# Batch 0's second feed-forward product as seven products, row-block pair by row-block pair

## The chip, the cores and the metric

The kernel runs on one core of a Trainium2 chip. The metric is the device time of one execution in microseconds. Before the change it is 704.37 us, the median of 3 runs (704.09 to 704.53). The profiled execution took 704.29 us; its span in the trace is 702.5 us, with TensorE's clock granted at 0.998 throughout.

## What is computed

```python
# x: (8, 8, 512, 64), state: (8, 8, 32, 64), float32
scores  = scale * x @ state^T          # per batch and head: 512 x 32
a       = softmax(scores)
xread   = a @ state                    # 512 x 64
scores2 = scale * state @ x^T          # 32 x 512
sread   = softmax(scores2) @ x         # 32 x 64
t = concat([xread, sread], axis=2)     # (8, 8, 544, 64)
t = t.transpose(0, 2, 1, 3).reshape(8 * 544, 512)
h = t @ w_in                           # w_in: (512, 2048)
g = h / (1 + exp(-1.702 h))
out = g @ w_out                        # w_out: (2048, 512)
```

The weights arrive as 64-bit floats and are rounded to 32 bits in the kernel. Everything else is 32-bit.

## The kernel before the change, in words

**Engines.** Each engine takes its instructions strictly in the order in which the code emits them. There is no scheduler: the order was written out by hand. TensorE does the products, VectorE (DVE in the profile) most of the element-wise work, ScalarE (ACT) the activations and most copies out of PSUM, and SyncE (SP) issues all transfers.

**Weights.** `PIECES` lists 32 pieces, 16 of w_in and then the 16 row blocks of w_out (128 rows by 512 columns, loaded as pairs of words). Piece *i* is loaded by `load_weight`. The row blocks of w_out use the four rooms of `later` in turn, so block piece *i*+4 can only be loaded when piece *i* has been rounded. Rounding builds the 32-bit number from the two words. Its VectorE steps are `mask` (L214: the exponent bits), a clamp and shift of these (L222 and L223, for w_out), `fraction` (L232), and in `round_b` the sign (L243), the low word (L246) and the final product (L250). For w_in the clamp is two ScalarE activations instead (L225 and L226), up to `AHEAD` = 3 pieces ahead. For w_out no step is taken ahead of its piece.

**Batches 0 and 1** are interleaved, since the weights are still arriving. For a quarter *c* of the 2048 columns, `att_M` multiplies w_in with the state (L327), and `up_x` multiplies the result with the normalized scores (L539) and applies the activation on ScalarE (L542), one block *f* of 128 columns at a time: blocks 0 to 15 of both batches.

**Batch 0's second product** is the loop over *f* at L1302. Each turn rounds row block *f* of w_out and then runs `down` for the four row groups: four products of 128 x 128 with 128 x 512 (L557), added up in four PSUM banks over the 16 turns. Between turns stand the state reads (`att_eT`, `att_sread`, `att_srT`), two `att_M`, and the last eight `up_x` of batch 1. Each row group is then copied out by ScalarE (L564) and stored.

**Batches 1 to 7** take their second product in seven half-size products in place of eight (Winograd's form of Strassen's scheme). With the left matrix in quarters a11 to a22 and w_out in quarters B11 to B22, the sums are T1 = B12 - B11, T2 = B22 - T1, T3 = B22 - B12, T4 = B21 - T2 on the right (`T_of`, L1285), and S1 = a21 + a22, S2 = S1 - a11, S3 = a11 - a21, S4 = a12 - S2 on the left (`s12`, L580 and L581; `s3`, L586). `strassen_two` splits most of the seven once more (`strassen_low`, L703), with sums of quarters of quarters: `low_made` and `low_away` make those of the right side, the latter in a room that is then stored to DRAM (L663), and `low_third` (L1285 too) makes the third in place. For batch 1 the first two products, P1 and P2, are taken whole (L752), and the following P5 in parts. Into P1 and P2 of batch 1 the attention of batch 2 is hooked: its scores (L327 into the banks o_2 and o_3), their transposes (`att_blocks`, L358), maxima (`att_s_max`, L365 and L366) and exponentials (`att_s_exp`, L384, ScalarE).

So on VectorE the order after the last row block is: T1, the sums of quarters, S1, S2, T2, S3, T3, more sums of quarters, the transposes of batch 2's x (`turn_x`, L163), T4 and its sums, the sums of S1 and S2 (first seven of L759), the transposes and maxima of batch 2, and then the sum of P2 and P1 (next L759, `osb`), which frees the PSUM bank o_1 that the second part of P5 writes.

Of the kernel before, what the change touches and what calls it, by code (L numbers as in the profile page):

```python
# [10 lines left out]
FP32 = mybir.dt.float32  # L11
# [3 lines left out]
ALU = mybir.AluOpType  # L15
# [5 lines left out]
def kernel(  # L21
# [71 lines left out]
    def att_ps(shape, name):  # L93
        return psA.tile(shape, FP32, tag="att", name=name)
# [7 lines left out]
    free = [gpool.tile([P, 2, S], FP32, name=f"g_{i}") for i in range(HF)]  # L102

    sums = konst.tile([P, 3, HF * HN], FP32, name="sums")
    T1, T2, T4 = (sums[:, i].rearrange("p (f n) -> p f n", f=HF) for i in range(3))
    free += [
        sums[:, 1 + i // 2, 2 * S * (i % 2) : 2 * S * (i % 2 + 1)].rearrange("p (k t) -> p k t", k=2) for i in range(4)
    ]
    later = konst.tile([P, 8, S], FP32, name="later")

# [59 lines left out]
    w_out = konst.tile([P, NF, DM], FP32, name="w_out")  # L170
    w_in_words, w_out_words = moe_w_in.bitcast(I32), moe_w_out.bitcast(I32)

    PIECES = [("i", c, k) for c in range(NFC) for k in range(NPR)] + [("o", f) for f in range(NF)]
    raw, power, begun = {}, {}, {}
    AHEAD = 3

# [39 lines left out]
    def round_a(i):  # L216

        if i not in power:
            mask(i)
        sc = power[i]  # L220
        if PIECES[i][0] == "o":
            nc.vector.tensor_scalar(sc, sc, most, least, ALU.min, ALU.max)  # L222
            nc.vector.tensor_scalar(sc, sc, -least, 8.0, ALU.add, ALU.mult)  # L223
            return
        nc.scalar.activation(out=sc.bitcast(FP32), in_=sc, func=AF.Relu, bias=edge[0], scale=-8.0)  # L225
        nc.scalar.activation(out=sc, in_=sc.bitcast(FP32), func=AF.Relu, bias=edge[1], scale=-1.0)  # L226
# [8 lines left out]
    def round_b(i, ahead, follows):  # L235


        if i not in begun:
            fraction(i)
        dst = begun.pop(i)  # L240
        lo, hi = words(i)
        sc = power.pop(i)
        nc.vector.scalar_tensor_tensor(sc, hi, -0x80000000, sc, ALU.bitwise_and, ALU.bitwise_or)  # L243
        powers_to(ahead)

        nc.vector.scalar_tensor_tensor(dst, lo, 2.0**-32, dst.bitcast(I32), ALU.mult, ALU.add)  # L246
        del raw[i]
        if follows and i + 1 in raw:
            fraction(i + 1)
        nc.vector.scalar_tensor_tensor(dst, dst, 2.0**-20, sc.bitcast(FP32), ALU.mult, ALU.mult)  # L250
# [19 lines left out]
    def round_to(n, ahead=AHEAD):  # L270

        nin = NFC * NPR
        while done["b"] < min(n, len(PIECES)):
            i = done["b"]
            powers_to(i + 1)
            round_b(i, min(i + 1 + ahead, max(nin, i + 1)), i + 1 < nin and (i + 1 < n or i >= NPR))
            done["b"] += 1
            while done["b"] > NPR and done["load"] < len(PIECES) and before(done["load"]) < done["b"]:
                load_weights(done["load"] + 1)
# [80 lines left out]
    def att_s_max(b):  # L360
        a = A[b]
        a["mx2"] = []
        for g in range(NG):
            mx = apool.tile([P, 1], FP32, tag="mx2", name=f"mx2_{b}_{g}", bufs=4)
            nc.vector.tensor_reduce(out=mx, in_=a["s"][g], axis=AX.X, op=ALU.max, negate=True)  # L365
            nc.vector.tensor_scalar(mx, mx, scale, None, ALU.mult)  # L366
            a["mx2"].append(mx)
# [164 lines left out]

    G = {}

    def up(key, f, ntok, lhs, rhs, spare=False):
        hps = att_ps([P, ntok], f"h_{key}_{f}") if spare else psH.tile([P, ntok], FP32, tag="h", name=f"h_{key}_{f}")
        n = len(lhs)
        for i in range(n):
            nc.tensor.matmul(hps, lhs[i], rhs[i], start=(i == 0), stop=(i == n - 1))  # L539
        if f % 2 == 0:  # L540
            G[key, f // 2] = free.pop(0)
        nc.scalar.activation(out=G[key, f // 2][:, f % 2, :ntok], in_=hps, func=AF.Gelu_apprx_sigmoid)  # L542

    def up_x(b, f, spare=False):
        c, o = divmod(P * f, FC)
        m = A[b]["M", c]
        up(b, f, S, [m[:, g, o : o + P] for g in range(NG)], [A[b]["aT"][:, g] for g in range(NG)], spare)

    O = {}

    def down(key, r, fs, dst, last):

        if fs[0] == 0:
            O[key, r] = bank_o[r]
        ops = O[key, r]
        for f in fs:
            nc.tensor.matmul(  # L557
                ops, G[key, f // 2][:, f % 2, P * r : P * (r + 1)], w_out[:, f], start=(f == 0), stop=(f == NF - 1)
            )
            if last and f < HF and f % 2:  # L560
                free.append(G.pop((key, f // 2)))
        if fs[-1] == NF - 1:
            osb = opool.tile([P, DM], FP32, tag="osb", name=f"osb_{key}_{r}")
            nc.scalar.copy(osb, ops)  # L564
            nc.sync.dma_start(dst, osb)


    S1, S2 = (later[:, 4 * i : 4 * i + 4].rearrange("p f n -> p (f n)").rearrange("p (f t) -> p f t", f=HF) for i in range(2))

# [632 lines left out]
    def rounds(n):  # L1202
        round_to(done["b"] + n)
# [47 lines left out]
    def turn(b, c, then, n=()):  # L1251

        for i in range(nper):
            if i == nper - 1 and then:
                att_M(*then)
            up_x(b, nper * c + i)
            if i < len(n):
                rounds(n[i])
# [4 lines left out]
    round_to(3 * NPR)  # L1263
    turn(1, 1, (0, 2), [1, 1])
    round_to(4 * NPR)
    att_s_max(0)
    att_s_max(1)
    turn(0, 2, (0, 3))
    room = apool.tile([P, NPR, S], FP32, tag="xT", name="e2_01")
    att_s_exp(0, room[:, :NG])  # L1270
    att_s_exp(1, room[:, NG:])
    rounds(1)
    att_s_norm(0)
    att_s_norm(1)
    up_x(0, 3 * nper)
    up_x(0, 3 * nper + 1)
    up_x(0, 3 * nper + 2, True)
    up_x(0, 3 * nper + 3, True)
    rounds(1)


    B11, B12, B21, B22 = (w_out[:, HF * i : HF * (i + 1), HN * k : HN * (k + 1)] for i in range(2) for k in range(2))
# [15 lines left out]
        low_keep(k, room)  # L1298


    rest = list(range(2 * nper, NF))
    for f in range(NF):  # L1302
        rounds(1)
        round_to(NFC * NPR + f + 1)
        if f == NF - 1:

            up_x(1, rest.pop(0))
        for r in range(SCH):
            down(0, r, [f], out_x[0, r], r == SCH - 1)
        if f == 0:  # L1310
            for b in range(2):
                for g in range(NG):
                    att_eT(b, g)
        if f == 1:

            att_sread(0)
            att_sread(1)
            att_M(1, 2, True)
            att_M(1, 3)
        if f == 2:  # L1320
            att_srT(0)
            att_srT(1)
        if f == 2 or f % 2 == 1 and 1 < f < NF - 1:
            up_x(1, rest.pop(0))
        if f == HF:
            load_state(2)
            load_x_squares(2)
        if f == NF - 2:
            T_of(T1, B12, B11)
            low_away(6, B22)  # L1330
            low_made(5, T1, 1)
            for u in range(NU - 1):
                s12(1, u, S)
            T_of(T2, B22, T1)
            low_third(T1)
            for u in range(NU - 1):
                s3(1, u, S)
            T_of(B12, B22, B12)
            low_away(3, T3)
            low_third(T3)  # L1340
        if f == NF - 1:
            turn_x(2)
            low_made(2, T2, 0)
    s12(1, NU - 1, S)
    s3(1, NU - 1, S)

    def out_of(b):
        return lambda r, n: out_x[b, r, :, n].rearrange("r q n -> q r n")

    for b in range(1, B):  # L1350
        if b > 1:
            ahead = {"P1.1": [(up_strassen(b, S, *parts_x(b), A[b]["sums"]), ())]}
            if b == 2:
                ahead["P1.5"] = [low_sums(B21, low_a)[2], (low_keep, (1, turn_rooms[0]))]
                ahead["P1.6"] = [(low_third, (B21,))]
        else:
            ahead = {
                "P1a": [(low_third, (B22,)), (T_of, (T4, B21, T2)), (low_third, (T2,)), (low_away, (4, T4)), (low_third, (T4,))]
            }
        if b + 1 < B:  # L1360
            hooks = hooks_next(b + 1)
        else:

            steps, left, right = sr_sums()
            order = (
                ("P5.6", 2), ("P6.1", 3), ("P6.3", 6), ("P6.4", 7), ("P7.5", 8), ("P7.6", 9), ("P4.1", 16, 17), ("P4.5", 18, 19),
            )
            hooks = {name: [steps[i] for i in n] for name, *n in order}
            hooks["P3.7"] = [(low_third, (T1,))]
            beside = steps[10:16] + [(low_third, (t,)) for t in (B11, B21, T2, T3, T4, B22)]  # L1370
            ahead["P2.1"] = [steps[i] for i in (0, 1)]
            ahead["P2.3"] = [steps[i] for i in (4, 5)]
        for name, first in ahead.items():
            hooks[name] = first + hooks.get(name, [])
        a4 = {}

        at = hooks.setdefault("run", [])
        k = 3 if b + 1 < B else 0
        at[k:k] = [(low4_load, (a4,))]
        strassen_two(b, out_of(b), hooks, a4)  # L1380
        if b + 2 < B:
            load_state(b + 2)
            load_x_squares(b + 2)
# [35 lines left out]
```

## Time and profile before

| what | busy or time |
|---|---|
| span | 702.5 us |
| TensorE matmul | 689.3 us, 98% |
| VectorE | 569.4 us, 81% |
| ScalarE | 301.9 us, 43% |
| rounding of w_out on VectorE | 66.6 to 130.1 us of the span |
| batch 0's second product on TensorE | 78.2 to 153.3 us of the span |
| first part of P5 of batch 1 on TensorE | 170.05 us of the span |

The busy share of TensorE is an average over stages: an engine that is busy 98% of the whole span is not by that the only one that limits each stage, so the stage that changes has to be read by itself. Times below are counted from the start of the span. A 32-bit matmul is two records in the trace, so a turn of the loop at L1302 (4 matmuls) shows as 8 records.

### The profile page before, as it was taken

What the parts mean: (1) busy time and instruction counts of PE and PEld (TensorE: products, weight loads), DVE (VectorE), ACT (ScalarE), POOL (GpSimd) and SP (SyncE); (2) the same over time, 40 slices, a digit from 0 to 9 for tenths busy, and PEclk for the clock granted to TensorE, in tenths of its full rate; (3) what the DMA queues carried; (4) which work ended last, traced back from release to release, by engine and by line L of the source; (5) the groups of instructions that cost most, each with busy time, mean ns of one, the idle gap of its engine ahead of it and who ended that gap; (6) DMA issues with size and microseconds to landing.
All of it is one profiled execution on the core that took longest, in us unless ns stands there. A gap on an engine that the chain in (4) does not pass through costs nothing.

```text
span 702.5 us, 13525 instructions
## 1 busy us (share of the span) xinstructions
PE 689.3 (98%) x5263; PEld 560.1 (80%) x5263; DVE 569.4 (81%) x1187; ACT 301.9 (43%) x677; POOL 0.8 (0%) x8
## 2 busy tenths in 40 slices
PE   8989999999999999999999999999999999999996
PEld 3433444457998799889989899889988998999995
DVE  6999799998879989697969886988878795887540
ACT  5686520014336533654355533753375236422420
POOL 0000000000000000000000000000000000000000
PEclk9999999999999999999999999999999999999999
DMA  8921246326524484427451664157433840251001
GB/s 220 383 67 56 91 151 151 123 80 200 172 75 94 140 239 141 88 66 235 146 115 31 174 218 116 24 134 231 142 55 106 235 142 16 71 148 53 16 0 31
DMA packets 105807, 87.39 MB, mean 124 GB/s; under 512 B 64784, under 2 KB 84752, under 8 KB 105744
## 3 DMA queue, kind: packets, MB, share of 16 engines
q1 hardware_dynamic: 105744, 86.53, 42.0%
q8 instruction: 42, 0.69, 0.4%
q14 instruction: 21, 0.17, 0.1%
HBM read 68.94 MB, written 17.56 MB: 123 GB/s over the span
## 4 chain that ended last, share of the span: by engine, by line
PE 89%; DVE 6%; DMA 2%; SPq 1%; ACT 1%; issue 0%; DVEq 0%; ACTq 0%
PE low L703 28%; PE o L703 15%; PE o L1123 13%; PE o L557 8%; PE h L539 7%; PE upx L1123 5%; PE M L327 4%; PE o L600 2%; PE o L752 2%; PE upw L1123 2%; PE sr L515 1%; PE upx_sr L1123 1%; DMA w_out<-in_moe_w_in_dram 1%; DMA out_dram<-osb_sr 1%; PE o L327 1%; SPq L148 1%
## 5 line engine op out<-in xcount | busy, mean ns | idle before, releaser
L703 PE MATMUL low<-w_out,g 128*128 128x128 f32 x416 | 54.3, 276 | 0.0
L703 PEld LDWEIGHTS low<-w_out,g 128*128 128x128 f32 x416 | 50.5, 192 | 4.5 <-issue 3.4
L1123 PE MATMUL o<-ta,M 128*128 128x256 f32 x192 | 49.9, 382 | 0.0
L1123 PE MATMUL upx<-aT,M 128*128 128x256 f32 x192 | 49.3, 379 | 0.0
L703 PE MATMUL low<-low,g 128*128 128x128 f32 x336 | 43.3, 275 | 0.4 <-ACT o L712 0.4
L703 PEld LDWEIGHTS low<-low,g 128*128 128x128 f32 x336 | 40.3, 192 | 0.5 <-ACT o L712 0.5
L1123 PEld LDWEIGHTS o<-ta,M 128*128 128x128 f32 x192 | 35.5, 190 | 6.0 <-ACT g L1169 1.6
L1123 PEld LDWEIGHTS upx<-aT,M 128*128 128x128 f32 x192 | 36.0, 190 | 4.7
L542 ACT ACTIVATE g<-h 128x512 f32<-128x512 f32 x24 | 14.0, 591 | 54.5 <-PE h L539 54.5
L474 ACT COPY M<-M 128x512 f32<-128x512 f32 x59 | 30.7, 596 | 14.8 <-PE M L327 14.7
L703 PE MATMUL low<-sums,later 128*128 128x128 f32 x280 | 35.8, 275 | 0.0
L1129 ACT ACTIVATE g<-o 128x512 f32<-128x512 f32 (+1 forms) x56 | 31.3, 559 | 10.2 <-PE o L1123 10.2
L703 PEld LDWEIGHTS low<-sums,later 128*128 128x128 f32 x280 | 33.6, 192 | 0.1
L327 PE MATMUL M<-w_in,stT 64*32 64x512 f32 x472 | 32.0, 594 | 0.0
L539 PE MATMUL h<-low,M 128*128 128x512 f32 x64 | 29.5, 597 | 1.7 <-DVE low L420 1.7
L1123 PE MATMUL o<-ta,ms 128*128 128x256 f32 x120 | 30.8, 379 | 0.0
L539 PE MATMUL h<-aT,M 128*128 128x512 f32 x64 | 28.7, 599 | 1.4 <-ACT M L474 1.4
L557 PE MATMUL o<-w_out,g 128*128 128x512 f32 x64 | 28.5, 594 | 0.0
L557 PE MATMUL o<-w_out,sums 128*128 128x512 f32 x64 | 28.3, 592 | 0.0
L1129 ACT ACTIVATE g<-g 128x512 f32<-128x512 f32 (+1 forms) x28 | 16.8, 600 | 23.4 <-DVE g L1132 23.4
L539 PEld LDWEIGHTS h<-aT,M 128*128 128x128 f32 x64 | 11.8, 190 | 18.3 <-issue 12.2
L1169 ACT COPY g<-o 128x512 f32<-128x512 f32 (+1 forms) x28 | 15.5, 554 | 24.4 <-PE o L1123 24.4
(259 smaller groups left out, 1590.8 us busy)
## 6 DMA issues: line engine op xcount, KB each, us to landing
low<-low SPq DMA_DIRECT2D x108, 256.0 KB, 3.6
low<-low SPq DMA_DIRECT2D x11, 768.0 KB, 4.6
later<-in_moe_w_out_dram SPq DMA_DIRECT2D x16, 512.0 KB, 3.6
w_out<-in_moe_w_in_dram SPq DMA_DIRECT2D x12, 512.0 KB, 6.0
xsq<-in_x_dram SPq DMA_DIRECT2D x96, 64.0 KB, 2.3
xn<-in_x_dram SPq DMA_DIRECT2D x12, 512.0 KB, 4.8
out_dram<-osb SPq DMA_DIRECT2D x18, 256.0 KB, 2.2
out_dram<-later SPq DMA_DIRECT2D x14, 256.0 KB, 2.1
```

Of the source, the lines that this page charges most:

```text
L148: nc.sync.dma_start(xn[b][:, c], x_v[b, c])
L327: nc.tensor.matmul(ps[g][st], A[b]["stT"][rows, st], rhs(rows, j), start=True, stop=True)
L474: nc.scalar.copy(m[:, g], ps[g])
L539: nc.tensor.matmul(hps, lhs[i], rhs[i], start=(i == 0), stop=(i == n - 1))
L542: nc.scalar.activation(out=G[key, f // 2][:, f % 2, :ntok], in_=hps, func=AF.Gelu_apprx_sigmoid)
L557: nc.tensor.matmul(ops, G[key, f // 2][:, f % 2, P * r : P * (r + 1)], w_out[:, f], start=(f == 0), stop=(f == NF - 1))
L600: nc.tensor.matmul(ps[:, r], lhs[f][:, P * r : P * (r + 1)], rhs[:, f], start=(first and r == 0 and f == 0), stop=(f == HF - 1), skip_grou ...
L703: nc.tensor.matmul(ps, lhs[f], rhs[:, f], start=(first and f == 0), stop=(f == QF - 1), skip_group_check=True)
L752: nc.tensor.matmul(ps[:, r], lhs[f][:, P * r : P * (r + 1)], rhs[:, f], start=(r == 0 and f == 0), stop=(f == HF - 1), skip_group_check=True,)
L1123: nc.tensor.matmul(ps[:, k], lhs[i][:, o : o + P], rhs[i], start=(first and k == 0 and i == 0), stop=(i == n - 1), skip_group_check=True,)
L1129: nc.scalar.activation(out=dst, in_=src, func=AF.Gelu_apprx_sigmoid)
L1169: nc.scalar.copy(c12, Y(u))
```

## The change

Batch 0's second product is also taken as seven products. The 16 row blocks of w_out form 8 pairs (block *f* and block *f*+8), loaded in the order 4, 12, 5, 13, 6, 14, 7, 15, 0, 8 and so on. When a pair has been rounded, eight VectorE subtractions and additions of 128 x 256 make the sums for this pair alone (`pair_sums`), and TensorE adds the pair's share to seven PSUM banks, two matmuls of 128 x 256 for each of the seven products (`pair`): P1 and P2 first, which need no sums, then the block of batch 1's `up_x`, then P6, P5, P7, P3 and P4 (`late`). T1, T2, T4 and T3 of w_out, which batch 1 needs in any case, come out of the same subtractions. At the end seven VectorE additions and one ScalarE copy combine the seven banks into the four quarters of the output, where the kernel before had four copies.

With it go: for 14 of the 16 row blocks the clamp moves from VectorE to ScalarE, one piece ahead; batch 0's blocks 8 to 11 of `up_x` are written out with the first two masks and clamps between them; the state reads of both batches stand together after the first pair's P1 and P2; and the eight last `up_x` of batch 1 share one PSUM bank, one in each of pairs 2 to 7 and two at the end. The purpose is to spare TensorE an eighth of this product's columns, and VectorE the clamps.

```diff
@@ sums
-    T1, T2, T4 = (sums[:, i].rearrange("p (f n) -> p f n", f=HF) for i in range(3))
+    T1 = sums[:, 0].rearrange("p (f n) -> p f n", f=HF)
+    T24 = sums[:, 1:].rearrange("p i (f k n) -> p (i f) k n", f=HF // 2, k=2)
+    T2, T4 = T24[:, :, 0], T24[:, :, 1]
...
-    PIECES = [("i", c, k) for c in range(NFC) for k in range(NPR)] + [("o", f) for f in range(NF)]
+    PIECES = [("i", c, k) for c in range(NFC) for k in range(NPR)] + [("o", HF * k + (f + HF // 2) % HF) for f in range(HF) for k in range(2)]
...
@@ round_a
-        if PIECES[i][0] == "o":
+        if i in (NFC * NPR + 2, NFC * NPR + 3):
             nc.vector.tensor_scalar(sc, sc, most, least, ALU.min, ALU.max)
             nc.vector.tensor_scalar(sc, sc, -least, 8.0, ALU.add, ALU.mult)
             return
@@ round_to
-            round_b(i, min(i + 1 + ahead, max(nin, i + 1)), i + 1 < nin and (i + 1 < n or i >= NPR))
+            round_b(i, min(i + 1 + ahead, i + 2 if i >= nin else nin), i >= nin or i + 1 < nin and (i + 1 < n or i >= NPR))
...
     round_to(4 * NPR)
+    nin = NFC * NPR
+    mask(nin)
+    mask(nin + 1)
     att_s_max(0)
     att_s_max(1)
-    turn(0, 2, (0, 3))
+    powers_to(nin + 1)
+    up_x(0, 2 * nper)
+    powers_to(nin + 2)
+    up_x(0, 2 * nper + 1)
+    up_x(0, 2 * nper + 2)
+    att_M(0, 3)
+    up_x(0, 2 * nper + 3)
     room = apool.tile([P, NPR, S], FP32, tag="xT", name="e2_01")
     att_s_exp(0, room[:, :NG])
     att_s_exp(1, room[:, NG:])
-    rounds(1)
+    rounds(3)
     att_s_norm(0)
     att_s_norm(1)
...
+    def pair_sums(i):
+        f = ORDER[i]
+        a11, a12, a21, a22 = a_of(f)
+        s1, s2, s4 = s_of(i)
+        t2, t4 = t24(i)[:, 0], t24(i)[:, 1]
+        steps = [
+            (s1, a21, a22, ALU.add), (T1[:, f], B12[:, f], B11[:, f]), (s2, s1, a11), (t2, B22[:, f], T1[:, f]),
+            (a21, a11, a21), (t4, B21[:, f], t2), (s4, a12, s2), (B12[:, f], B22[:, f], B12[:, f]),
+        ]
+        for v in steps if i else steps[::2] + steps[1::2]:
+            tt(*v)
+
+    def pair(i, *names):
...
+            for r in range(2):
+                nc.tensor.matmul(
+                    ps7[name][:, HN * r : HN * (r + 1)], lhs[:, P * r : P * (r + 1)], rhs,
+                    start=(i == 0 and r == 0), stop=(i == HF - 1), skip_group_check=True,
+                )
...
     rest = list(range(2 * nper, NF))
-    for f in range(NF):
-        rounds(1)
-        round_to(NFC * NPR + f + 1)
...
-        for r in range(SCH):
-            down(0, r, [f], out_x[0, r], r == SCH - 1)
...
+    for i in range(HF):
+        round_to(nin + 2 * i + 2)
+        if i == 0:
+            pair(i, "P1", "P2")
+            for b in (1, 0):
                 for g in range(NG):
                     att_eT(b, g)
+            round_to(nin + 4)
+            att_sread(1)
             att_sread(0)
             att_M(1, 2, True)
             att_M(1, 3)
...
+            pair_sums(i)
             att_srT(0)
             att_srT(1)
...
+        else:
+            pair_sums(i)
+            pair(i, "P1", "P2")
+        if i > 1:
+            up_x(1, rest.pop(0), bank=up_bank)
+        late()
+        if i == HF // 2:
             load_state(2)
             load_x_squares(2)
-        if f == NF - 2:
-            T_of(T1, B12, B11)
...
-            T_of(T2, B22, T1)
...
-            T_of(B12, B22, B12)
...
+    low_away(6, B22)
+    low_made(5, T1, 1)
+    for u in range(NU - 2):
+        s12(1, u, S)
...
+    nc.scalar.copy(k1, ps7["P1"])
+    tt(osb, ps7["P2"], k1, ALU.add)
+    put_out(0, 0, osb)
+    tt(k2, ps7["P6"], k1, ALU.add)
+    tt(t01, ps7["P5"], k2, ALU.add)
+    tt(k3, ps7["P7"], k2, ALU.add)
+    tt(k1, ps7["P7"], t01, ALU.add)
+    put_out(1, 1, k1)
+    tt(t01, ps7["P3"], t01, ALU.add)
+    put_out(0, 1, t01)
+    tt(k3, ps7["P4"], k3, ALU.add)
+    put_out(1, 0, k3)
+    for f in rest:
+        up_x(1, f, bank=up_bank)
+    for i, t in enumerate(t_room):
+        nc.scalar.copy(sums[:, 2, 2 * S * i : 2 * S * (i + 1)], t.rearrange("p n k t -> p (n k t)"))
+    s12(1, NU - 2, S)
+    low_third(T1)
+    for u in range(NU - 1):
+        s3(1, u, S)
+    low_away(3, T3)
+    low_third(T3)
+    turn_x(2)
+    low_made(2, T2, 0)
     s12(1, NU - 1, S)
     s3(1, NU - 1, S)
...
-                "P1a": [(low_third, (B22,)), (T_of, (T4, B21, T2)), (low_third, (T2,)), (low_away, (4, T4)), (low_third, (T4,))]
+                "P1a": [(low_third, (B22,)), (low_third, (T2,)), (low_away, (4, T4)), (low_third, (T4,))]
```

## The prediction

> **What bounds the kernel now.** I read the page's first part, then the busy time by stretches around the change, then the timelines of VectorE, TensorE and ScalarE there.
>
> ```profile
> PE 689.3 (98%) x5263; PEld 560.1 (80%) x5263; DVE 569.4 (81%) x1187; ACT 301.9 (43%) x677; POOL 0.8 (0%) x8
> ```
>
> Over the whole span TensorE looks like the only bound. By stretches (length, then PE, PEld, DVE, ACT busy), from the first w_out rounding of the loop to its end, and from there to batch 1's P5:
>
> ```profile
> 77.20:130.10 52.90, 52.66 (x288) 24.67 (x287) 51.35 (x106) 10.39 (x22) 0.00 (x0) 1.00 0.47 131
> 130.10:170.30 40.20, 40.20 (x171) 23.36 (x170) 38.99 (x54) 8.74 (x15) 0.00 (x0) 1.00 0.39 146
> ```
>
> Here VectorE is as full as TensorE: 97% in both. The rest is the gap between dependent instructions. The VectorE timeline (start, length) of the last row block, and of the end of its queue:
>
> ```profile
> 126.58 0.42 DVE L214 TENSOR_SCALAR low<-later 128x512 int32<-128x512 int32 x1
> 127.03 0.43 DVE L222 TENSOR_SCALAR low<-low 128x512 int32<-128x512 int32 x1
> 127.50 0.43 DVE L223 TENSOR_SCALAR low<-low 128x512 int32<-128x512 int32 x1
> 127.84 0.42 DVE L232 TENSOR_SCALAR w_out<-later 128x512 int32<-128x512 int32 x1
> 128.18 0.68 DVE L243 SCALAR_TENSOR_TENSOR low<-later,low 128x512 int32<-128x512 int32 x1
> 128.78 0.68 DVE L246 SCALAR_TENSOR_TENSOR w_out<-later,w_out 128x512 f32<-128x512 uint32 x1
> 129.50 0.69 DVE L250 SCALAR_TENSOR_TENSOR w_out<-w_out,low 128x512 f32<-128x512 f32 x1
> 130.11 2.28 DVE L1285 TENSOR_TENSOR sums<-w_out 128x2048 f32<-128x2048 f32 x1
> ...
> 169.66 0.15 DVE L366 TENSOR_SCALAR mx<-mx 128x1 f32<-128x1 f32 x1
> 170.30 0.69 DVE L759 TENSOR_TENSOR osb<-o,g 128x512 f32<-128x512 f32 x1 [0.49 <-PE o L752]
> ```
>
> A row block takes 3.53 us (126.58 to 130.11). From there the queue runs without a pause to 169.8, and then waits 0.49 us for TensorE. So VectorE's whole slack in this stage is half a microsecond. Who waits for that `osb`? TensorE's timeline:
>
> ```profile
> 136.02 7.03 PE L557 MATMUL o<-w_out,sums 128*128 128x512 f32 x16
> 142.89 1.88 PE L539 MATMUL h<-low,M 128*128 128x512 f32 x4
> ...
> 156.75 7.07 PE L752 MATMUL o<-w_out,g 128*128 128x256 f32 x32
> ...
> 171.05 1.16 PE L703 MATMUL o<-low,spare_M 128*128 128x128 f32 x8
> ```
>
> The product at 171.05 writes bank o_1, which `osb` has just read (170.30 + 0.69 = 170.99). The next one (172.10) needs a ScalarE copy that is queued behind batch 2's exponentials, and these wait for the VectorE maxima. So VectorE's time at 170 is TensorE's time.
>
> **What the Trainium skill says.** "VectorE: DVE Perf Modes", in the section on the TRN2 errata, puts a 32-bit `tensor_tensor` at (N+151)/0.96 ns, a fixed part per instruction: 424 ns for 256 columns. The trace agrees (L759 128x256: 418 ns), so cutting T1 to T4 into 8 pieces each costs more than it looks. "TensorE: Matmul & The Clock Gate", section LDWEIGHTS, gives P/1.2, 107 ns for 128 columns. The trace has 190 ns here, and that is what I use. "Perfetto Trace Analysis", section Optimization Strategy, warns that the most-contended engine changes between regimes: the stretches above show it.
>
> **TensorE's part.** 16 records of 128x512 take 6.87 us (chain of waits), 0.859 us a matmul; 32 of 128x256 take 6.91, 0.432 us a matmul. Removed: 64 x 0.859 = 55.0. Added: 7 products x 2 x 8 pairs = 112 x 0.432 = 48.4. Saved 6.6 us; 224 weight loads x 0.19 = 42.6 stay hidden. Walking the new queue from 78.20: P1 and P2 of pair 0 (1.73) to 79.9; the transposes of both batches with their waits to 82.5, as now (81.47 to 83.9); state reads and two `att_M` (3.8) to 86.2. Now there is no turn of the loop between, so srT waits for ScalarE's four copies of M (0.5 each from 85.3, to 87.4): 1.3 us new. Pair 0's other five products (4.32) to 91.9, pair 1 (6.05) to 97.9, six pairs of 6.05 + 1.72 = 7.77 to 144.5. Two `up_x` through one bank, the second waiting for the activation (0.9), to 148.8. Batch 1's P1 starts at 153.35 now: TensorE alone is 4.5 us ahead.
>
> **VectorE's work.** With the clamps on ScalarE a piece takes 2.475 us (w_in: L250 starts at 41.76, 44.24, 46.72). 14 x (3.53 - 2.475) = -14.8. The four whole subtractions go: 2.20 + 3 x 2.32 = -9.2. The pair sums: 64 x 0.335 (four L759 128x256 from 194.38 to 195.72) = +21.4. The seven sums at the end: 6 x 0.61 + 0.72 = +4.4. Net +1.8: the clamps pay for the pair sums, and nothing is left over.
>
> **The new wait.** The clamp of a pair's second block is emitted after the activation of the pair before, so on ScalarE it is queued behind an activation that waits for TensorE. From the start T of pair *i* on TensorE: P1 and P2 1.73, `up_x` to activation 1.92 (94.82 to 96.74), activation 0.49, the two clamps 0.76 + 0.72 (57.58, 58.33), signal 0.03: VectorE cannot begin the sign step of block 2i+3 before T + 5.65. The ScalarE rows behind these numbers:
>
> ```profile
> 57.58 0.71 ACT L225 ACTIVATE low<-low,edge 128x512 f32<-128x512 int32 x1
> 58.33 0.72 ACT L226 ACTIVATE low<-low,edge 128x512 int32<-128x512 f32 x1
> ...
> 96.74 0.60 ACT L542 ACTIVATE g<-h 128x512 f32<-128x512 f32 x1 [1.40 <-PE h L539]
> ```
>
> Behind it in VectorE's queue stand all later sums and blocks. VectorE comes to the first such block early: sums of pair 1 done at 88.1, pair 2 at 2.56 + 2.48 + 2.68 = 7.72 to 95.8, one block more to 98.3. The gate opens at 97.9 + 5.65 = 103.6. So 5.2 us of lead are lost, and never regained: 7.72 per pair against TensorE's 7.77. TensorE does not feel it yet (P2 of the next pair could begin at T + 8.63, the block is there at T + 8.25). The last gate is pair 6's: T = 97.9 + 4 x 7.77 = 129.0, so the last sign step is at 134.65. Now it is at 128.18: 6.5 us later.
>
> **From there to `osb`.** Now: 128.18 to 169.81, 41.6 us without a gap. New: 41.6 - 9.2 + one pair's sums 2.7 + the seven sums 4.4 = 39.5, so `osb` can start at 134.65 + 39.5 = 174.1, against 170.30. Then bank o_1 is free at 174.8 (+3.8), and the copy behind the exponentials, whose first maximum is ready 0.8 us before `osb` can start (169.02 now), comes at 173.4 + 2.4 = 175.8 (2.4: from exponential, 169.69, to the end of the copy, 172.05) against 172.1 (+3.7). TensorE, at the first part of P5 by 148.8 + 16.7 = 165.5, waits. After it VectorE has 2.2 us pauses (175, 181) and all work follows TensorE, so the shift stays: 704.37 + 3.8 = 708.2.
>
> **At nothing:** ScalarE's clamps (14 x 1.48, ScalarE busy 20%); its two copies of T2 and T4 (ready by 152, read at 159); the output stores (no reader). The last two row blocks are loaded behind batch 2's 18 loads (10 us of issue): about 127.5, just when their mask is due; 0 to 0.5 us, I take 0.
>
> **Rivals.** (A) The gate costs nothing, because VectorE still has other work there: `osb` 5.2 earlier, 168.9, product at 169.6 in place of 171.05: 702.9. For it: ScalarE is idle 80% here; against: its queue is in order, and the activation's input comes when it comes. (B) TensorE alone decides, VectorE's tail being hidden: 704.37 - 4.5 = 699.9. For it: 98% busy; against: the 0.49 us of slack. (C) Each pair is longer, because some seven VectorE instructions per pair now wait for another engine and none of the kernel before shows what that adds; at 0.06 us each, 0.42 a pair, over five pairs: 2.1 more, 710.3. (D) Parts of the lead survive and cancel: about 704.4.
>
> **How the numbers follow.** Main case 0.68, C 0.12, A 0.09, B 0.04, D 0.07. A lies at the 0.2% border (702.96), so half of it counts as faster, with B: 0.09. D and the rest of A: 0.12. Slower 0.79. Predicted is the main case, 708.2. The range leaves out A, B and part of D below (0.15), and C's end above (0.05): 704.5 to 710.5.
>
> **What would show it.** In the profile after: VectorE idle for about 5 us near 100, released by a ScalarE clamp; a period near 7.8 us per pair on TensorE; batch 1's P1 near 149; then TensorE idle of some 3 us at the second product of P5, released by VectorE's `osb`, near 175. Wrong if VectorE shows no such pause, if pairs take over 8 us, or if TensorE has no idle at P5.

## The result, and the profile after

The changed kernel takes 710.29 us (median of 4 runs, 709.82 to 710.79) against 704.23 us (703.75 to 704.53) for the kernel before, measured side by side: 1.0087 times as long, with a 95% interval of 1.0069 to 1.0104. It is slower by 6.06 us; the prediction had it slower by 3.8.

TensorE is indeed relieved (684.5 us of matmul where there were 689.3), and VectorE is a little busier. The two lines that follow are from the page of the changed kernel, its busy times and the row of TensorE's granted clock in 40 slices of the span, in tenths of full speed:

```profile
PE 684.5 (97%) x5357; PEld 580.1 (82%) x5359; DVE 573.5 (81%) x1226; ACT 321.1 (45%) x704; POOL 0.8 (0%) x8
PEclk9999999997999999999999999999999999999999
```

In the kernel before that row has a 9 in all 40 slices. Here one slice, the tenth (159 to 177 us), has a 7: something happens there to the clock itself.

The path that the prediction walked is there. In the timeline of VectorE (start, duration, engine, line, operation; in brackets the idle time just before and what ended it):

```profile
103.56 0.69 DVE L245 SCALAR_TENSOR_TENSOR low<-later,low 128x512 int32<-128x512 int32 x1 [5.24 <-ACT low L228]
...
134.61 0.69 DVE L245 SCALAR_TENSOR_TENSOR low<-later,low 128x512 int32<-128x512 int32 x1
...
174.17 0.69 DVE L747 TENSOR_TENSOR osb<-o,g 128x512 f32<-128x512 f32 x1
...
180.86 0.29 DVE L696 TENSOR_TENSOR spare_M<-low,spare_M 128x128 f32<-128x128 f32 x1 [4.07 <-PE low L691]
```

The first line is the sign step held up by a clamp on ScalarE (the gate), the second the last sign step of w_out, the third `osb`. ScalarE's timeline shows what the clamp (two instructions, L227 and L228) stood behind, an activation that waits for TensorE:

```profile
101.57 0.60 ACT L549 ACTIVATE g<-down_up 128x512 f32<-128x512 f32 x1 [8.43 <-PE down_up L546]
102.06 0.71 ACT L227 ACTIVATE low<-low,edge 128x512 f32<-128x512 int32 x1
102.81 0.72 ACT L228 ACTIVATE low<-low,edge 128x512 int32<-128x512 f32 x1
```

Now compare the last line of VectorE's timeline with its counterpart in the kernel before:

```profile
175.15 0.29 DVE L708 TENSOR_TENSOR spare_M<-low,spare_M 128x128 f32<-128x128 f32 x1 [2.23 <-PE low L703]
```

`osb` is 3.87 us late, and this later add on VectorE is 5.71 us late. Between the two VectorE waits for TensorE. So here is TensorE's timeline in the changed kernel, same columns:

```profile
148.88 3.62 PE L740 MATMUL o<-w_out,g 128*128 128x256 f32 x16
...
165.73 1.05 PE L691 MATMUL low<-sums,later 128*128 128x128 f32 x8
174.92 2.07 PE L691 MATMUL o<-low,spare_M 128*128 128x128 f32 x8 [8.13 <-DVE osb L747]
176.78 1.92 PE L691 MATMUL low<-low,spare_M 128*128 128x128 f32 x8
178.49 2.26 PE L691 MATMUL low<-sums,later 128*128 128x128 f32 x16
```

Line 165.73 is the first product of batch 1's P5: eight records in 1.05 us. The second product, 174.92, has the same eight records and takes 2.07, where the kernel before took 1.16 for it; the third takes 1.92. The third shows no wait in front of it: TensorE works, at half speed. The view of stretches shows it outright. Its columns are the length, then the busy time of PE, PEld, DVE, ACT and POOL, then PEclk, the share of DMA and GB/s:

```profile
166.80:168.90 2.10, 0.00 (x0) 0.00 (x0) 2.10 (x4) 0.00 (x0) 0.00 (x0) 1.00 0.82 263
168.90:174.90 6.00, 0.00 (x0) 0.00 (x0) 5.93 (x13) 2.72 (x4) 0.00 (x0) 0.50 0.69 214
174.90:179.10 4.20, 4.18 (x19) 4.18 (x20) 1.85 (x3) 1.41 (x5) 0.00 (x0) 0.50 0.49 94
179.10:185.00 5.90, 5.90 (x55) 5.90 (x54) 4.07 (x12) 1.04 (x4) 0.00 (x0) 1.00 0.81 223
```

TensorE becomes idle at 166.8. Two microseconds later its clock is granted at 0.50; when work resumes at 174.9 it stays there for 4.2 us more. Work that takes 4.2 us at half speed takes 2.1 at full speed. Of these 2.1 us some 0.3 don't show: in the kernel before the products here start 1.05 and 1.00 us apart (171.05, 172.10, 173.10), where later ones follow each other every 0.89 us, and these short pauses vanish behind the slow work. The sum is then 3.87 (`osb` late) + 1.84 (slow work) = 5.71 us at 181 us, and 6.00 at the last add of this kind in the span.

### The profile page after: what moved, and what is told of

Its sections match the earlier page's. It is cut to its first block, busy times and chain, and to the rows that moved or that the text cites. A ratio compares the mean times of both kernels' runs of the same rounds, so it can differ in the third digit from the quotient of the medians.

```text
span 708.5 us, 13782 instructions
## 1 busy us (share of the span) xinstructions
PE 684.5 (97%) x5357; PEld 580.1 (82%) x5359; DVE 573.5 (81%) x1226; ACT 321.1 (45%) x704; POOL 0.8 (0%) x8
## 4 chain that ended last, share of the span: by engine, by line
PE 85%; DVE 8%; ACT 3%; DMA 2%; issue 1%; SPq 0%; DVEq 0%; ACTq 0%
PE low L691 27%; PE o L691 15%; PE o L1111 13%; PE upx L1111 5%; PE h L546 5%; PE M L329 4%; PE o L1354 3%; PE o L588 2%; PE down L1354 2%; PE upw L1111 2%; PE o L329 1%; PE down_up L546 1%; PE sr L517 1%; PE warm L127 1%; DVE low L1281 1%; PE upx_sr L1111 1%
## 5 line engine op out<-in xcount | busy, mean ns | idle before, releaser
L1117 ACT ACTIVATE g<-o 128x512 f32<-128x512 f32 (+1 forms) x56 | 31.3, 559 | 10.2 <-PE o L1111 10.2
L691 PE MATMUL o<-low,spare_M 128*128 128x128 f32 x160 | 22.2, 283 | 8.1 <-DVE osb L747 8.1
L227 ACT ACTIVATE low<-low,edge 128x512 f32<-128x512 int32 x30 | 21.6, 719 | 13.9 <-DVE low L216 13.8
L691 PEld LDWEIGHTS o<-low,spare_M 128*128 128x128 f32 x160 | 20.3, 199 | 8.3 <-DVE osb L747 8.3
L1111 PEld LDWEIGHTS o<-ta,ms 128*128 128x128 f32 x120 | 22.8, 190 | 3.1
```

The lines of the kernel that those rows point to most:

```text
L691: nc.tensor.matmul(ps, lhs[f], rhs[:, f], start=(first and f == 0), stop=(f == QF - 1), skip_group_check=True)
L1111: nc.tensor.matmul(ps[:, k], lhs[i][:, o : o + P], rhs[i], start=(first and k == 0 and i == 0), stop=(i == n - 1), skip_group_check=True,)
L1117: nc.scalar.activation(out=dst, in_=src, func=AF.Gelu_apprx_sigmoid)
```

## The experiments

Two causes were to be told apart. **The gate**: VectorE's 5.2 us of idle time, lost to a clamp that is queued on ScalarE behind an activation, is what makes `osb` late. **The clock**: TensorE's long wait for `osb` brings its clock down, which costs 2 us over and above the wait. Rivals: longer pairs or VectorE's added work alone, and TensorE as the only bound.

### TensorE's wait filled with work

```diff
+        def warm():
+            ps = att_ps([P, FC], "idle")
+            for _ in range(9):
+                nc.tensor.matmul(ps, ident, w_in[0][:, 0], start=True, stop=True)
+        if key == 1:
+            first[1].append(warm)
```

> The changed kernel with nine extra matmuls of 128x512 (0.86 us each, results not used) put on TensorE right behind the first product of P5 in batch 1, so that its wait of 8.1 us for osb is filled with work. Nothing else is altered, and the wait itself still ends with osb at 174.2 us. Theory of the clock (TensorE's clock was 0.50 from 169.0 to 179.1 us in the trace of the changed kernel, which costs about 2.05 us once the work resumes at 174.9): the clock stays at 1.00, the second product of P5 still starts near 174.9, and the time falls by about 2 us, to 708.2 us. Rival (the remaining 2 us come from more work or more waits elsewhere, longer pairs for instance): the time stays at 710.3 us.

Measured: 708.46 us (707.26 to 709.89), 1.0058 [1.0046, 1.0070]. The page's clock is 1.00, and TensorE's timeline has the two products at their usual length, though they start as late as ever:

```profile
175.03 1.16 PE L691 MATMUL o<-low,spare_M 128*128 128x128 f32 x8 [0.39 <-DVE osb L747]
176.03 1.12 PE L691 MATMUL low<-low,spare_M 128*128 128x128 f32 x8
```

With more work for TensorE the kernel is 4.0 us slower than the one before (704.44 us beside these runs) and not 6.1: 2.0 us are won, as expected (the two intervals leave it open by some 1.5 us either way; the two profiled runs differ by 1.86). Waiting and the price of waiting are two things: the wait itself has the same end as before, and only its price went.

### The gate taken away: power bits two blocks ahead

```diff
-round_b(i, min(i + 1 + ahead, i + 2 if i >= nin else nin), ...)
+round_b(i, min(i + 1 + ahead, i + 3 if i >= nin else nin), ...)
```

The changed kernel makes a block's power bits (mask and clamp) one block ahead; here it is two. The text on record counts the block itself too, and so says three instead of two.

> The changed kernel with the power bits of w_out made three blocks ahead instead of two, so that the clamps of the next pair stand on ScalarE ahead of the activation behind which one of them waited; no work is added or removed. Theory of the gate (VectorE's 5.2 us of idle time at 98.3 us is what moves osb from 170.3 to 174.2): no idle time of VectorE near 98 us, osb starts at 174.2 - 5.2 = 169.0, the second product of P5 at about 169.6, 1.4 us ahead of the kernel before, and the time is 704.2 - 1.4 = 702.9 us; TensorE's wait there is 2.8 us, and if its clock falls in that as it did in 8.1 us, up to 2 us more, 704.9. Rival (VectorE's added work and not the gate makes osb late): the idle time only moves to another place, osb stays near 174 and the time near 710 us.

Measured: 706.90 us (706.48 to 708.27), 1.0039 [1.0027, 1.0051]; neither 702.9 nor 710. The idle time near 98 us is gone (0.18 us is left), but `osb` comes at 171.76, only 2.4 us earlier. VectorE's timeline shows the new wait in its place:

```profile
123.03 0.43 DVE L216 TENSOR_SCALAR low<-later 128x512 int32<-128x512 int32 x1 [2.65 <-DMA later<-in_moe_w_out_dram]
```

And the timeline of SyncE's queue (SPq) shows why that block is late:

```profile
109.86 8.72 SPq L159 DMA_DIRECT2D xsq<-in_x_dram  x16
118.69 0.95 SPq L194 DMA_DIRECT2D later<-in_moe_w_out_dram  x2
```

The last two loads of w_out are issued behind 16 loads of batch 2's x, which take SyncE 8.7 us. The gate had hidden that: a VectorE that is held up for 5 us doesn't notice a load that is 2.6 us late. TensorE's wait for `osb` was 5.12 us in this run, its clock at 0.50 from 172.3 to 175.7.

### The gate and the late loads taken away

```diff
         if i > 1:
+            powers_to(nin + 2 * i + 4)
             up_x(1, rest.pop(0), bank=up_bank)
...
-        if i == HF // 2:
+        if i == HF // 2 + 1:
             load_state(2)
             load_x_squares(2)
```

> The changed kernel with two edits. The power bits of the second block of the next pair are made just ahead of each pair's activation (the mask stands one instruction earlier on VectorE, its two clamps ahead of the activation on ScalarE), and the 18 loads of batch 2's state and squares are issued one pair later, so that the last two loads of w_out don't queue behind them on SyncE. Theory of the gate: VectorE has no idle time above 1 us between 84 and 150 us, osb starts at 174.2 - 5.2 = 169.0 us, the second product of P5 near 169.6, after a wait of TensorE of 2.8 us (1.4 us ahead of the kernel before): 702.9 us, and 704.5 us if the clock falls in the 2.8 us as it did for a wait of 2.05 us (about 1.6 us of cost). Rival (another wait takes the gate's place once more): osb at 171 us or later, 706 us or more.

Measured: 705.75 us (704.72 to 707.30, 20 runs), 1.0018 [1.0011, 1.0025]. VectorE's timeline:

```profile
98.20 0.68 DVE L245 SCALAR_TENSOR_TENSOR low<-later,low 128x512 int32<-128x512 int32 x1
...
141.44 0.69 DVE L1308 TENSOR_TENSOR osb<-o,s_room 128x512 f32<-128x512 f32 x1 [1.03 <-ACT s_room L1411]
...
170.39 0.69 DVE L747 TENSOR_TENSOR osb<-o,g 128x512 f32<-128x512 f32 x1
```

The sign step that stood at 103.56 stands at 98.20, without a wait: 5.4 us of lead are kept. One line of code ahead of an activation does that, with no work added. `osb` of batch 1 gains 3.8 us of it (expected 5.2): at 141.44 VectorE has caught up, and the final sums of batch 0 and a sum behind them wait 1.03 + 0.31 + 0.48 us. The first of these is a smaller gate of the same kind: ScalarE's copy of P1 (140.82 us) stands behind the last pair's activation (140.33 us), which waits for TensorE. What the copy would bring if it stood ahead of the activation was not tried. TensorE then waited 4.39 us for `osb`, its clock was 0.50 from 169.5 to 176.4, and by the next add in the table below the run had lost 2.3 us more. So with gate and late loads gone `osb` stands within 0.1 us of the kernel before: the gate accounts for the 3.8 us at `osb`, and the rest of the loss is the clock. The prediction had charged the gate with 5.2 us there and counted on a lead of 1.4 us beyond it, which the final sums take.

### `osb` ahead of batch 2's transposes, with and without the gate

```diff
-        at(p2, att_blocks, b)
-        at("P2a" if first else "P2.1", att_s_max, b)
-        p3 = "P2b" if first else "P2.3"
+        at("P2" if first else p2, att_blocks, b)
+        at("P2" if first else "P2.1", att_s_max, b)
+        p3 = "P5.4" if first else "P2.3"
```

With the gate, all else as in the changed kernel:

> The changed kernel, gate kept, with osb alone put ahead of the transposes and maxima of batch 2's scores on VectorE. Osb then starts near 174.2 - 2.9 = 171.3 us and the second product of P5 near 171.9: TensorE waits 5.1 us instead of 8.1. If its clock falls in 5.1 us as in 8.1 us, the time is 710.3 - 3.0 = 707.3 us with a second of slow work behind it of about 2 us; if it does not, 705.3 us. If osb is not what TensorE waits for: 710.3 us.

Measured: 709.58 us (708.00 to 709.87), 1.0065 [1.0053, 1.0077]. That is 2.3 us more than expected. `osb` came at 171.44 and TensorE's wait was 5.30 us, as expected, but the clock stayed at 0.50 until 177.7, so 5.5 us of work ran at half speed instead of 4.2, and another 0.32 us went to a ScalarE copy at 181.6. By the medians 0.9 of the 2.7 us gained at `osb` reached the end (5.1 us slower than the kernel before, in place of 6.1). The trace doesn't explain so much: the profiled execution is the quickest of the five (708.00 us), and in it 2.3 us reach the end. What the others lose in addition has no trace here.

With power bits two blocks ahead (and the late loads still there):

> As the run without the gate, and the add that makes osb in batch 1 is put on VectorE ahead of the transposes and maxima of batch 2's scores (2.9 us), whose exponentials on ScalarE come two products of P5 later; no work is added or removed. If VectorE's order alone decides when TensorE can start the second product of P5: osb near 166.1 us, the second product near 166.8, straight behind the first, no wait of TensorE there, no fall of its clock, and TensorE's saved 6.6 us less what it gave back before (its bound in the prediction) show: about 699.9 us. Rival (another wait stands behind osb: the exponentials, a transfer, a bank): TensorE idles by 1 to 3 us at another place of batch 1, and the time is 701 to 703 us.

Measured: 703.66 us (702.62 to 705.86, 14 runs), 0.9993 [0.9983, 1.0002], so no difference from the kernel before that this measurement shows. `osb` came at 168.93, not 166.1. VectorE waited 2.38 us for the late load here, but the run without late loads (all three edits, below) has `osb` only 1.2 us sooner, because the waits at the final sums come out in their place. The profiled execution took 705.69 us, 2 us more than the median; the stretches show that its clock fell:

```profile
167.60:169.70 2.10, 0.05 (x2) 0.04 (x1) 2.10 (x5) 0.25 (x1) 0.00 (x0) 1.00 0.94 331
169.70:170.80 1.10, 1.10 (x10) 1.10 (x11) 1.10 (x3) 0.00 (x0) 0.00 (x0) 0.98 1.09 356
170.80:174.20 3.40, 3.40 (x19) 3.40 (x18) 3.30 (x8) 0.53 (x2) 0.00 (x0) 0.50 0.20 68
```

TensorE idled 2.05 us, resumed at full clock, and only 1.1 us later fell to half, for 3.4 us. The wait is over when its price falls due.

### All three edits

Power bits ahead of the activation and batch 2's loads one pair later (the diff of the run without gate and late loads), and `osb` first (the diff above).

> The same two edits, and the add that makes osb ahead of the transposes and maxima of batch 2's scores. Theory: osb at 169.0 - 2.9 = 166.1 us, the second product of P5 straight behind the first, near 166.8, TensorE never idle by more than half a microsecond there, its clock at 1.00 throughout: the 6.6 us that TensorE saves come out less what the kernel before had lost there already, about 700 us, so faster than both kernels. Rival: a further wait (ScalarE's copies behind the exponentials, a bank) holds TensorE up; then 702 us or more.

Measured: 702.24 us (701.49 to 703.26), 0.9969 [0.9958, 0.9981]: faster than both kernels, by 2.1 us than the one before and by some 8 us than the changed one. In TensorE's timeline the second product of P5 starts 6.5 us sooner than in the changed kernel:

```profile
168.47 1.16 PE L691 MATMUL o<-low,spare_M 128*128 128x128 f32 x8 [1.57 <-DVE osb L747]
```

A wait of 1.57 us is left, for `osb` came at 167.73, and the clock stayed at 1.00. The expected 700 us took that wait as none.

Two runs tried to take this last wait. One put VectorE instructions into the pause at 141 us (three of 1.9 us in all; the text on record counts one too many):

> The version without gate, with late loads of the squares and with osb ahead of the transposes, and four instructions of VectorE (2.6 us) that wait for no product (one of T1's own sums, three of the left factor's third sums) placed ahead of batch 0's final sums, where VectorE was idle for 1.0 us at 141.6 (and 0.8 us more by 157). Theory: the idle time is filled, osb starts at 167.7 - 1.0 to 1.8, that is 165.9 to 166.7 us, TensorE's wait of 1.57 us in front of the second product of P5 falls to 0.5 us or nothing, and the time from 702.2 to 701 us. Rival (the final sums come later by as much as is filled, and what waits for their banks on TensorE loses it): no change or slower.

Measured: 702.18 us (701.33 to 703.87), 0.9971 [0.9962, 0.9981]: nothing. The first of them overwrites a part of T1 that TensorE's P5 of the last pair still reads, so VectorE waited 1.64 us for TensorE there, and `osb` came at 167.62, 0.1 us sooner. The pause that was to be filled ends with ScalarE's copy of P1, and the product that the filling waited for was done 0.6 us later, so this filling could not use it. The other put one extra matmul into the wait of 1.57 us:

> The version with all edits (702.24 us), in which TensorE waits 1.57 us for osb and its clock stayed at 1.00, with one extra matmul of 128x512 (0.86 us) in that wait. Theory of the clock: the wait is too short to bring the clock down, so filling it is worth nothing: 702.2 us, within 0.7. Rival (every wait costs more than its length): 701 us or less.

Measured: 702.00 us (701.33 to 702.29), 0.9962 [0.9950, 0.9975]: no change, as expected of a wait that had not brought the clock down.

### The wait filled once more, without the gate

The version with gate and late loads taken away, and five extra matmuls in TensorE's wait of 4.39 us (the first diff with 5 in place of 9).

> The version without gate and with late loads of the squares (705.75 us; TensorE waited 4.39 us for osb, its clock was 0.50 from about 169.5 to 176.4 us, 5.3 us of that with work), with five extra matmuls of 128x512 (0.86 us each, results not used) in TensorE's wait. Theory of the clock: no fall of the clock there, the second product of P5 still near 171.1, and the time lower by half of 5.3, about 2.6 us: 703.1 us. Rival (the clock falls for another reason than TensorE's idle time): no change, 705.7 us.

Measured: 705.71 us (704.48 to 706.37, 21 runs), 1.0017 [1.0011, 1.0024]: no change at all, though the page's clock is 1.00. This needs the trace. The table gives, for the `osb` adds on VectorE, how much later than in the kernel before each starts (worked out from the rows of both timelines; times of the kernel before in the head).

| us later than before | 170.30 | 200.78 | 245.72 | 470.50 | 697.92 |
|---|---|---|---|---|---|
| changed kernel | 3.87 | 5.71 | 5.52 | 6.59 | 6.00 |
| changed, wait filled | 3.98 | 3.88 | 3.69 | 4.74 | 4.14 |
| no gate, no late loads | 0.09 | 2.40 | 2.21 | 3.05 | 2.44 |
| no gate, no late loads, wait filled | 0.27 | 0.18 | -0.01 | 2.24 | 1.63 |
| all three edits | -2.57 | -2.06 | -2.25 | -2.19 | -2.77 |

From the first to the second column is the price of the clock: 1.84 us in the changed kernel and 2.31 without the gate, and nothing in both once the wait is filled. (The last row gives back 0.5 us there with the clock at 1.00.) But without the gate the gain is given back between 245 and 470 us. The view of waits of that run has, for TensorE from 240 to 430 us (us in total, times, longest):

```profile
PE low L691 <- DMA low<-low: 1.4, 2, 0.9
```

Here TensorE waits for sums that are read back from HBM; the same run without the filling has 0.6 us of such waits in that stretch. That is 0.8 of the 1.4 us more that this profiled run loses there. What makes these transfers late was not tried; it stays open. The profiled pair also shows more to win than most executions had: the 20 executions without the filling list mean clocks of 0.993 to 0.997, the profiled one (706.72 us) 0.993, while all 21 with the filling list 0.998 to 1.000, as the kernel before does. So the filling kept the clock up, and why the medians agree all the same is explained only in part. In the changed kernel the same filling kept 1.86 us to the end.

### Single parts: the clamps

All clamps back on VectorE in the changed kernel (the condition in `round_a` is `PIECES[i][0] == "o"` again):

> The changed kernel with one part undone: all clamps of w_out on VectorE again, as in the kernel before. The gate (5.2 us) goes with it, VectorE gets 14.8 us more. Theory (VectorE's queue alone decides when osb is made): osb at 174.2 + 14.8 - 5.2 = 183.8 us, TensorE loses 9.6 us more, shared between the pairs and the second product of P5: 719.9 us, up to 2 us more where the clock falls in other waits. Rival (the clamps on ScalarE only cost, since one of them is the gate): 705 us or less.

Measured: 716.83 us (716.38 to 717.67), 1.0176 [1.0163, 1.0190]; `osb` at 180.97. So the move of the clamps is worth 6.4 us (12.5 us slower than the kernel before, in place of 6.1) to the changed kernel in spite of the gate that it brings. Expected were 9.6, at `osb` too, which came 6.8 us later than in the changed kernel: in this order the two clamps take VectorE 0.93 us per block (mask and both clamps 1.26 us, from 119.68 to 120.94, the mask alone 0.33) and not the 1.06 that the prediction read off the kernel before; that is 1.8 us over 14 blocks, and the remaining 1.0 at `osb` was not traced.

The clamps on ScalarE in the kernel before, and nothing else:

```diff
-        if PIECES[i][0] == "o":
+        if i in (NFC * NPR + 2, NFC * NPR + 3):
             nc.vector.tensor_scalar(...)
```

> The kernel before with one part of the change alone: the clamps of 14 of w_out's 16 blocks on ScalarE instead of VectorE. VectorE is relieved of 14.8 us, ScalarE gets some 20 us. Theory (before, TensorE is never idle by more than 1.2 us after 50 us, so VectorE's relief is worth nothing by itself, and a clamp that waits behind an activation there costs at most VectorE's lead): 704.2 us, within 0.7 us. Rival (VectorE's work, 81% of the span, bounds the second product of batch 0): up to several us faster. If ScalarE's clamps gate VectorE also here beyond its lead: slower, 706 us or more.

Measured: 721.85 us (720.86 to 722.72), 1.0246 [1.0232, 1.0260]. This expectation failed badly. The kernel before makes no power bits ahead for w_out, so each sign step waits for a clamp that was only just asked for, and every second clamp stands behind an activation of `up_x` as well: the two lines from VectorE's timeline repeat with the same waits from 110 to 145 us.

```profile
123.88 0.69 DVE L243 SCALAR_TENSOR_TENSOR low<-later,low 128x512 int32<-128x512 int32 x1 [1.99 <-ACT low L226]
127.78 0.69 DVE L243 SCALAR_TENSOR_TENSOR low<-later,low 128x512 int32<-128x512 int32 x1 [1.21 <-ACT low L226]
```

So VectorE needs 8.59 us for two blocks, where it needed 7.06. To tell the two causes apart, the same with one block ahead (`i + 2 if i >= nin else nin` in place of `max(nin, i + 1)`), as the change has it:

> The kernel before with the clamps of 14 blocks of w_out on ScalarE, as in the run of that part alone, and in addition with the power bits of each block made one block ahead (there every sign step of VectorE waited 1.2 to 2.5 us for its own clamp, since the kernel before makes none ahead). Theory of the gate (a clamp queued behind an activation of up_x on ScalarE waits for TensorE's product of that up_x): the last sign step of w_out is held to the activation that TensorE's place in batch 0's products sets, 144.8 us by the trace of the kernel before, so near 147 us instead of 128.2; osb comes some 17 to 19 us later than 170.3, the time is 720 to 723 us. Rival (only the latency of the clamps made the other run slow, and making them one ahead hides it): 704 us, with VectorE relieved for nothing.

Measured: 717.35 us (717.08 to 719.39), 1.0197 [1.0183, 1.0211]; less than the 720 to 723 expected, and far from 704. ScalarE's timeline shows the gate bare:

```profile
130.79 0.60 ACT L542 ACTIVATE g<-h 128x512 f32<-128x512 f32 x1 [4.05 <-PE h L539]
131.28 0.71 ACT L225 ACTIVATE low<-low,edge 128x512 f32<-128x512 int32 x1
132.03 0.72 ACT L226 ACTIVATE low<-low,edge 128x512 int32<-128x512 f32 x1
```

ScalarE idles 4.05 us with a clamp in its queue, because an activation that waits for TensorE stands ahead of it. VectorE's sign step follows at 132.78, after 3.28 us of idle time, and so every 8.58 us, which is TensorE's time for two turns of the loop and one `up_x`, and the pace of the run above too. So the latency of the clamps was worth some 4.5 of that run's 17.5 us, and the gate sets the pace in both. Making a clamp "ahead" doesn't help if it is emitted behind the activation.

## Why the prediction was right, and where it fell short

**Right, to some two tenths of a microsecond, up to the second product of P5.** TensorE at batch 1's P1: 148.8 predicted, 148.88 measured. The gate: opening at 103.6, 103.56; idle time 5.2, 5.24. Last sign step: 134.65, 134.61. `osb`: 174.1, 174.17. First part of P5: 165.5, 165.73. End of the copy behind the exponentials: 175.8, 175.46 + 0.32. Pairs: 7.77 us, and the sign steps of the trace are 7.76 apart. The run without gate and late loads confirms the gate as the cause of the 3.8 us (with the gate alone gone, the late load takes part of its place), and those of the kernel before with the clamps moved show the mechanism by itself.

**The step that failed** is the last one: "all work follows TensorE, so the shift stays: 704.37 + 3.8 = 708.2". The shift did not stay; it grew from 3.87 to 5.71 us within the next products, because TensorE resumed at half its clock. The missing term is the price of TensorE's wait, 1.84 us in the trace, and 2.0 by the times of the run that filled it. Everything else that happens up to the end adds some 0.3. That the measured time lies within the stated range, 0.2 us below its end, is luck in part: the end was set for rival (C), longer pairs, and the main case had 3.8 of the 6.06 us.

The numbers to see it coming were in the prediction. It has TensorE reach the first part of P5 by 165.5, a product of about 1 us, and bank o_1 free for the second at 174.8, which is a wait of over 8 us; yet its list of what to look for says "some 3 us", which was never worked out. The trace has 8.13. And it drew on "TensorE: Matmul & The Clock Gate" in the Trainium skill for its section LDWEIGHTS alone, while that page's Part 1, The HAM clock gate, says that the half-speed clock is the default and that activity in a free-running window of 3413 ns lifts it. The traces here agree with the window: the clock stayed at half for 3.4 us (two blocks ahead, with and without `osb` first), 6.8 (without gate and late loads; gate kept, `osb` first) and 10.2 us (changed kernel; clamps on VectorE), one, two and three times such a window.

**The rivals.** (C), longer pairs, named 710.3, which is what was measured, but by luck: the trace refutes its reason, for pairs take 7.76 us. (A), the gate costs nothing, and (B), TensorE alone decides, are refuted by 710.29 itself; what (A) would have been is the run without gate and late loads, and even that doesn't reach 702.9, since 1.8 us of VectorE's lead go at the final sums and the clock still falls. (D), parts of the lead survive, did not come true either: TensorE is 4.5 us ahead at P1 (148.88 against 153.35), and 3.87 us behind at the second product of P5.

**At nothing:** it is their place in ScalarE's queue that makes the clamps cost something; that ScalarE's time for them is missed anywhere, no run shows. The last two loads of w_out, put at 0 to 0.5 us, cost nothing in the changed kernel; 2.65 us came out as soon as the gate was gone.

## What to carry to other kernels

A short instruction moved to an idle engine inherits that engine's queue: look at what stands ahead of it and what that waits for, since 1.5 us of clamps held VectorE up for 5.2 us behind an activation, and placing the same clamps ahead of it freed the lead. When a shift moves a wait onto TensorE, write the length of that wait down and price the clock as well as the wait: here waits for `osb` of 2.05 to 8.16 us left 3.2 to 5.7 us of work at half speed behind them, half of which is lost, while one of 1.57 us left none, and one of 2.48 us neither, because of when it came. And take waits away one at a time with the trace in hand, because each one hides the next (the gate hid a late load, and that hid the pause at the final sums), and what is won early can be lost again to transfers later.

## What was not expected of the hardware

TensorE's clock fell to 0.50 about 2.1 us after the wait of 8.13 us began, but after a wait of 2.05 us it fell only 1.1 us after work had resumed, and after one of 5.12 us about when work resumed (172.3). The granted clock as the traces list it puts these together. Within each of the 14 traces all changes of the clock lie a whole number of 3.413 us apart, the window that the page named above gives, so each trace can be divided into such windows, and TensorE's idle time counted in each:

| run | wait of TensorE (us) | window (us) | idle in it (us) | clock after it |
|---|---|---|---|---|
| changed kernel | 8.13 | 165.49 to 168.90 | 2.11 | 0.50 |
| power bits two blocks ahead | 5.12 | 165.48 to 168.89 | 1.51 | 1.00 |
| the same, next window | 5.12 | 168.89 to 172.31 | 3.41 | 0.50 |
| two blocks ahead, `osb` first | 2.05 | 167.34 to 170.76 | 2.05 | 0.50 |
| all three edits | 1.57 | 166.42 to 169.83 | 1.57 | 1.00 |
| kernel before, clamps on ScalarE, one block ahead | 2.48 | 179.56 to 182.97 | 1.58 | 1.00 |
| the same, next window | 2.48 | 182.97 to 186.38 | 0.90 | 1.00 |

The last two rows are one wait of 2.48 us, longer than the 2.05 us that brought the clock down, and it cost nothing, for it lay across the end of a window. The product behind it runs at its usual length:

```profile
183.87 1.16 PE L703 MATMUL o<-low,spare_M 128*128 128x128 f32 x8 [2.48 <-DVE osb L759]
```

All 14 traces together, some 2700 windows from 50 us on, agree: behind windows with 1.84 us of idle time or less the clock stayed, behind those with 2.04 us or more it fell, at the window's end. Between the two nothing was measured. The clock came back at the end of windows with at most 0.20 us of idle time, and not behind those with 1.12 us or more. The page speaks of at least one idle window, about 3.4 us; here about 60% of a window was enough, so the measurement decides.

Where the windows lie the kernel doesn't set, so a short wait can cost something in one execution and nothing in the next. If a wait of 2.05 us must lie wholly in one window, an estimate from these numbers is (3.41 - 2.05) / 3.41, or 0.4 of the executions, and 0.5 if 1.84 us of it are enough. The run with that wait fits: nine of its 14 executions took 702.62 to 704.11 us with mean clocks of 0.998 to 1.000, and five took 705.21 to 705.86 with 0.997 (one with 0.998), which no execution of the kernel before beside them shows (0.998 to 1.000). Only one of the five is profiled, so that the clock is what parts them is likely and not shown.
